# Short matmuls on ones in TensorE's early waits, and column sums spread by TensorE, in a windowed-attention and MoE kernel

## The chip, the core and the metric

One core of a Trainium2 chip runs the whole program. TensorE (PE) multiplies, VectorE (DVE), ScalarE (ACT) and GpSimd (POOL) copy and compute elementwise, and SyncE's queue (SP) issues every DMA. The metric is the device time of one execution in microseconds (us), taken as the median of several. The times of the kernel before are 317.78, 322.66 and 318.96 us, median 318.96.

## The reference

Eight sequences of 576 tokens, eight heads of 64, window 32; then a layer with a squared ReLU whose bias adds a constant times the column sums of `w_out`:

```python
scores = q @ k.T / 8;  scores = where(|i - j| <= 32, scores, -1e9)
x = softmax(scores) @ v            # (8, 8, 576, 64) -> (4608, 512)
h = x @ w_in                       # 512 -> 2048
g = s * relu(h)**2 + b
out = g @ w_out                    # 2048 -> 512
    # = s * (relu(h)**2 @ w_out) + b * column_sums(w_out)
```

## The kernel before

**Order of the work.** Each operation is added to a graph (`_Graph.add`) with an engine, a cost, a key (its due time), what it reads and what it writes. `plan` is a list scheduler: it takes the operation that can start first, then the smaller key, and so writes out one fixed order for each engine; `emit` adds the semaphore waits. On the chip each engine keeps its order, whatever the real times are. So a change of a key, of a cost or of the engine of one copy moves other instructions too.

**Stages.** The first sequence's q and k come in pairs of heads (`load_pair`, L685), are cast (L713), turned by TensorE (L733), copied out of PSUM (L740), and scored (L990) over a bank that was first filled with the mask (`opened`, L1009). Exponentials are taken on ScalarE (L1034). V of the first sequence comes as rows (L624), is cast (L629), and put in place by TensorE with a 0/1 matrix (`place_rows`, L643, in 32-row tiles); the copies out of PSUM are L651/L652. The product with V (`joint`, L915), the normalisation (reciprocal L939, multiply L941), TensorE's transposes (L948) and the copies to XT (L956) end a unit of 128 rows. Sequence 1 goes much the same way (L720, L749, L755, L990, L1020). From sequence 2 on, q and k are loaded whole (`piece`, L798), cast by GpSimd (L806), turned by transposing DMAs (L813), and k is put in order by GpSimd (L823); v is loaded at L607 and cast at L615/L616; the scores are L857.

**The layer.** `s1` (L1185) multiplies a block of tokens with `w_in`, whose eight loads (L579) GpSimd casts (L582), into one of the two banks of W; ScalarE's ReLU (L1192) and VectorE's square (L1194) make GT. The blocks are 224, 128, 160, 256, 256 and then 512 tokens. `early` (L1234) multiplies the first 512 tokens with `w_out` piece by piece, as it arrives, into both banks of O and both of AVN; the later blocks do so in `s2` (L1203). `put` (L1219, L1223) scales by s, adds the vector CVEC = b times the column sums of `w_out`, and stores. The bank of an accumulator is free again only after `put` has read it.

**Column sums.** `colsum` (L1244) lets TensorE multiply ones with `w_out` in four 32-column tiles, so that W's second bank holds the sums of columns 128x to 128x+127 on each of the partitions 32x to 32x+31. One operation of VectorE (L1249) scales them by b into a spare buffer, and 16 copies of 32x128 (L1255 on ScalarE, 4; L1256 on VectorE, 12) spread them to CVEC's 128x512. `put` of the first 512 tokens waits for all 16.

**Before any data** five matmuls of 512 columns on ones run (L528); nothing fills TensorE's later waits.

Of the kernel before, what the change touches and what calls it, by code (L numbers as in the profile page):

```python
# [13 lines left out]
H = 8  # L14
# [3 lines left out]
NPAIR = H // 2  # L18
# [7 lines left out]
SPLIT = (2, 3)  # L26
VROWS = NPAIR
PLACED = NPAIR
WHOLE = 9
SPREAD = ('act', 'dve', 'dve', 'dve')  # L30
# [6 lines left out]
TURNKEY = -20.5  # L37
TURN = (None, 0)
FIRST = ((None, 0), (0, 0), (1, 0), (0, 1), (1, 2), (1, 1), (2, 0), (0, 2), (0, 3), (2, 1), (1, 3), (2, 3), (2, 2), (None, 0), (None, 0), (None, 0), (None, 0))
# [3 lines left out]
HELD = (1800.0, 2800, 700.0, 3600)  # L43
OPEN = -23.1
REST = ('dve', 'dve')
ORDER1 = (('p', 0), ('p', 1), ('w', 0), ('w', 1), ('p', 2), ('p', 3), ('v', 0), ('w', 2), ('w', 3), ('e', 0), ('v', 2), ('v', 3), ('v', 4), ('v', 1))
XTS = 3000.0
ROWS = 4
BODY = 128 * ROWS
XPE = 20  # L50
PACE = ((-1, -1, -1),) * 3
# [3 lines left out]
SLACK = (2000.0, 1500.0, 4500, 4000)  # L55
# [9 lines left out]
COPYK = (('act', 'dve', 'act', 'dve'), ('act', 'act', 'dve', 'dve'))  # L65
XTE = ('act', 'act', 'dve', 'act', 'dve', 'act', 'dve', 'dve', 'act', 'act', 'act', 'act', 'act', 'act', 'dve', 'act', 'act', 'act', 'dve', 'act')
TURN1 = (0, 3, 0, 1, 0, 1, 0, 0, 1)
SCORE1 = ('O', 'O', 'SC', 'SC')
FIRSTQK = (('qk', 'qk', 'kq', 'qk'), ('qk', 'qk', 'kq', 'kq'))
K1 = ('act', 'dve', 'dve', 'pool')  # L70
Q1 = ('pool', 'pool', 'dve', 'dve')
# [6 lines left out]
class _Task:  # L78
    __slots__ = ("n", "stream", "fns", "cost", "lat", "key", "deps", "users", "left",
                 "ready", "start", "fin", "dma", "sem", "seq", "val", "used", "snap", "slack", "after", "next", "half", "mark", "form")  # L80

    def __init__(self, n, stream, fns, cost, lat, key, dma, slack, after, form):
        self.form = form
        self.slack, self.after, self.next = slack, after, []
        self.n, self.stream, self.fns, self.cost, self.lat, self.key, self.dma = \
            n, stream, fns, cost, lat, key, dma
        self.deps, self.users = set(), []
        self.ready = self.start = self.fin = 0.0
        self.sem = self.seq = self.val = None
        self.used = False  # L90
        self.snap = self.half = self.mark = None


class _Graph:
# [12 lines left out]
    MARGIN, FROM = 250.0, -20.05  # L107
    RING, PUSH, CALM, ISSUE, WRITE = 112.0, 95.0, 40.0, 1400.0, 600.0
# [6 lines left out]
    def add(self, stream, fns, cost, reads=(), writes=(), key=0.0, accum=False, dma=None, waits=(),  # L115
            late=0.0, slack=0.0, form=None):
# [18 lines left out]
        t.deps.discard(t)  # L135
        for r in reads:
            self.readers.setdefault(r, []).append(t)
# [9 lines left out]
    def plan(self):  # L147
# [112 lines left out]
        while any(rings.values()):  # L260
            done, clock[0] = serve(rings, clock[0], 1e9)
            done.fin = clock[0] + self.WRITE

# [92 lines left out]
def bass_sliding_window_symmetric__then__act_starrelu_kernel(  # L356
# [13 lines left out]
    sizes = [224, 128, 160, 256, 256]  # L370
# [9 lines left out]
    with ExitStack() as es:  # L380
# [54 lines left out]
        SROW = sb((128, 2), F32, "srow")  # L435

# [56 lines left out]
        def due(c, u):  # L493
            tok = c * S + unit_rows(c, u)[0]
            blk = next(x for x in range(NM) if TBLK[x][0] + TBLK[x][1] > tok)
            f = (tok - TBLK[blk][0]) / TBLK[blk][1]
            before = PH[blk] - PH[blk - 1] if blk > 0 else 4.0
            return PH[blk] - 14.0 - (1.0 - f) * before
# [5 lines left out]
        add("dve", lambda e: e.memset(ONESW[:], 1.0), 150, writes=["ONESW"], key=-99)  # L504
        add("dve", lambda e: e.memset(RECS[:], 1.0), 250, writes=[("REC", i) for i in range(NU)], key=-58)
# [134 lines left out]
        def place_rows(us, key, waits=()):  # L640
# [6 lines left out]
                60.0 + 110.0 * H, form="row", reads=[("VN", 0), ("VN", 1), "PICK"],  # L647
# [21 lines left out]
        def place_tail(waits):  # L669
# [6 lines left out]
                skip_group_check=True) for x in (0, 1)], 300.0, reads=[("NAT", ni), "IDENT"], writes=[res], key=-20.4, waits=waits)  # L676
# [48 lines left out]
        def turn_pair(b, name, pr, key, banks, eng, slack):  # L725
# [3 lines left out]
            if b == 0:  # L729
# [5 lines left out]
                    300.0, form="64", reads=[("NAT", ni), "IDENT"], writes=[res], key=key)  # L735
# [270 lines left out]
        def opened(name, bank, key, waits):  # L1006
# [5 lines left out]
                waits=waits)  # L1012
# [45 lines left out]
        def joint(b, us, key, waits=()):  # L1058
# [6 lines left out]
                    slack=1500.0, waits=waits)  # L1065
# [108 lines left out]
        def s1(m, f0):  # L1174
# [16 lines left out]
                writes=[("W", wb)], key=key, slack=XTS)  # L1191
# [50 lines left out]
        def colsum():  # L1242
# [4 lines left out]
                1050, form="column", reads=["ONESW"] + [("Wout", i, x) for i in range(4) for x in (0, 1)], writes=[("W", 1)], key=-12.0)  # L1247
            some = OUTS[NOUT - 1][:, 0:128]
            add("dve", lambda e: e.tensor_scalar(some, W[:, 1, 0:128], SB128[:, 1:2], None, ALU.mult),  # L1249
                250, reads=[("W", 1), ("SB128", 1)], writes=[("OUTS", NOUT - 1)], key=-12.0)  # L1250
            for y in range(4):
                for x in range(4):
                    to, part = CVEC[32 * y:32 * y + 32, 128 * x:128 * x + 128], some[32 * x:32 * x + 32, :]
                    eng = SPREAD[y]
                    add(eng, (lambda e, to=to, part=part: e.copy(to, part)) if eng == "act" else  # L1255
                        (lambda e, to=to, part=part: e.tensor_copy(to, part)), {"act": 300, "dve": 200}[eng],  # L1256
                        reads=[("OUTS", NOUT - 1)], writes=[("CVEC", x // 2, y)], key=P2[0] + 0.5)
# [281 lines left out]
```

## Time and profile before

| | |
|---|---|
| median of three executions | 318.96 us |
| the profiled execution, device time | 318.48 us |
| its span, first to last instruction | 316.7 us |
| outside the span | 1.78 us |
| mean granted TensorE clock | 0.978 |
| PE, DVE, ACT, POOL busy | 304.4, 189.5, 143.1, 105.6 us |
| moved by DMA | 56.10 MB |

The profile is of one execution. A row of the timeline has the start in us, the busy time, the engine, the line, the operation, output and inputs, shapes and count; in square brackets the idle time before it and what ended that. A row of the windows has the busy time of each engine in that stretch with the number of instructions, and at the end the granted TensorE clock, the mean share of the DMA engines in use, and GB/s. A row of the chain of waits has start, duration, engine and line.

### The profile page before, as it was taken

Reading aid. Unit: us, or ns where it says so; the run is one execution under the profiler, and the core shown is the slowest. Engines: PE = TensorE matmul, PEld = TensorE weight load, DVE = VectorE, ACT = ScalarE, POOL = GpSimd, SP = SyncE. Lnnn points to the kernel's source line nnn. Section 1 sums busy time; section 2 is a strip of 40 time slices with the busy share of each in tenths; the row PEclk is TensorE's granted clock in tenths of the full one; section 3 lists DMA queues with packets and bytes.
Section 4 is the critical chain, followed back from the end, with each engine's and each line's share of the span. In section 5 each row is a group of like instructions: output and inputs, shape, how many; then the busy total and the mean of one; then the engine's idle time right before and its main releaser. Section 6 shows DMA issues by size and latency. Waiting matters only on the chain.

```text
span 316.7 us, 8119 instructions
## 1 busy us (share of the span) xinstructions
PE 304.4 (96%) x3446; PEld 162.3 (51%) x3446; DVE 189.5 (60%) x375; ACT 143.1 (45%) x227; POOL 105.6 (33%) x125
## 2 busy tenths in 40 slices
PE   7799999949999999999999999999999999999995
PEld 3449875637764455454444444444444444444444
DVE  5457785596766867688448655776755543333312
ACT  4726676314744663665136524743544333333300
POOL 4258544661164336626334470266100000000000
PEclk9859999989999999999999999999999999999999
DMA  7999999994799899599999989996521110000022
GB/s 229 369 385 334 339 277 295 147 177 150 254 169 147 279 218 193 148 296 167 149 213 252 194 157 290 252 163 114 151 87 52 52 46 33 35 33 34 34 101 69
DMA packets 97974, 56.10 MB, mean 177 GB/s; under 512 B 70992, under 2 KB 88144, under 8 KB 97936
## 3 DMA queue, kind: packets, MB, share of 16 engines
q1 hardware_dynamic: 97936, 55.56, 74.6%
q8 instruction: 28, 0.46, 0.7%
q14 instruction: 10, 0.08, 0.1%
HBM read 36.70 MB, written 9.44 MB: 146 GB/s over the span
## 4 chain that ended last, share of the span: by engine, by line
PE 91%; DVE 3%; DMA 2%; ACT 1%; SPq 1%; issue 1%
PE w L1185 39%; PE o L1203 35%; PE avn L915 4%; PE o L1234 2%; PE avn L1234 2%; PE sc L857 2%; DVE cvec L1256 2%; DMA stg<-in_q_dram 2%; PE avn L643 1%; PE avn L948 1%; PE o L915 1%; PE sc L915 1%; SPq L685 1%; DVE outs L1219 1%; PE w L749 1%
## 5 line engine op out<-in xcount | busy, mean ns | idle before, releaser
L1185 PE MATMUL w<-xt,win 128*128 128x512 bf16 (+4 forms) x768 | 142.7, 328 | 0.1
L1192 ACT ACTIVATE r<-w 128x512 bf16<-128x512 f32 (+2 forms) x148 | 86.5, 586 | 104.8 <-PE w L1185 88.6
L1194 DVE TENSOR_TENSOR gt<-r 128x512 bf16<-128x512 bf16 (+2 forms) x148 | 81.5, 562 | 72.9 <-ACT r L1192 72.1
L1203 PE MATMUL o<-wout,gt 128*128 128x512 bf16 (+1 forms) x528 | 124.4, 373 | 0.0
L1185 PEld LDWEIGHTS w<-xt,win 128*128 128x128 bf16 x768 | 68.6, 99 | 54.1 <-ACT r L1192 1.8
L1203 PEld LDWEIGHTS o<-wout,gt 128*128 128x128 bf16 x528 | 50.4, 98 | 55.2 <-DVE gt L1194 0.5
L806 POOL CAST nat<-stg 128x1024 bf16<-128x1024 f32 (+1 forms) x36 | 39.8, 1105 | 59.9 <-DMA stg<-in_q_dram 45.8
L823 POOL COPY kt<-ktr 128x512 bf16<-128x512 bf16 (+1 forms) x30 | 30.7, 1022 | 28.4 <-DMA ktr<-nat 27.0
L885 ACT ACTIVATE ex<-sc 128x1024 bf16<-128x1024 f32 (+1 forms) x28 | 28.7, 1024 | 25.1 <-PE avn L915 24.0
L1219 DVE SCALAR_TENSOR_TENSOR outs<-o,sb,cvec 128x512 f32<-128x512 f32 (+1 forms) x35 | 25.5, 732 | 18.8 <-PE o L1203 18.6
L889 DVE TENSOR_TENSOR ex<-ex,mask 128x1024 bf16<-128x1024 bf16 (+1 forms) x28 | 21.1, 753 | 1.5 <-ACT ex L885 0.5
L941 DVE TENSOR_TENSOR xn<-avn,rec 128x512 bf16<-128x512 f32 (+1 forms) x30 | 20.7, 689 | 0.8
L915 PE MATMUL avn<-vb,ex 64*64 64x65 bf16 x912 | 19.2, 197 | 0.1
L915 PEld LDWEIGHTS avn<-vb,ex 64*64 64x64 bf16 x912 | 12.5, 106 | 12.4 <-issue 9.8
L857 PE MATMUL sc<-qt,kt 64*64 64x128 bf16 x432 | 11.4, 216 | 0.0
L616 POOL CAST vb<-vst 128x512 bf16<-128x512 f32 x13 | 9.0, 692 | 6.9 <-DMA vst<-in_v_dram 6.2
L939 DVE RECIPROCAL rec<-avn 128x8 f32<-128x8 f32 (+1 forms) x30 | 6.0, 200 | 7.6 <-PE avn L915 7.4
L582 POOL CAST wout<-stg 128x1024 bf16<-128x1024 f32 x7 | 7.5, 1075 | 6.0 <-DMA stg<-in_moe_w_out_dram 5.8
L1234 PE MATMUL avn<-wout,gt 128*128 128x512 bf16 x32 | 9.2, 380 | 0.0
L582 POOL CAST win<-stg 128x1024 bf16<-128x1024 f32 x8 | 8.4, 1046 | 2.0 <-DMA stg<-in_moe_w_in_dram 1.8
L616 DVE CAST vb<-vst 128x512 bf16<-128x512 f32 (+1 forms) x18 | 8.0, 446 | 0.0
L1234 PE MATMUL o<-wout,gt 128*128 128x512 bf16 x32 | 7.7, 380 | 0.0
(123 smaller groups left out, 155.3 us busy)
## 6 DMA issues: line engine op xcount, KB each, us to landing
out_dram<-outs SPq DMA_DIRECT2D x35, 256.0 KB, 2.9
vst<-in_v_dram SPq DMA_DIRECT2D x28, 256.0 KB, 6.4
stg<-in_k_dram SPq DMA_DIRECT2D x6, 1024.0 KB, 10.8
stg<-in_q_dram SPq DMA_DIRECT2D x6, 1024.0 KB, 5.8
stg<-in_moe_w_in_dram SPq DMA_DIRECT2D x8, 512.0 KB, 9.3
stg<-in_moe_w_out_dram SPq DMA_DIRECT2D x8, 512.0 KB, 6.3
stg<-in_q_dram SPq DMA_DIRECT2D x4, 288.0 KB, 4.9
stg<-in_k_dram SPq DMA_DIRECT2D x4, 288.0 KB, 5.1
```

Source lines behind the costliest of these rows:

```text
L806: add(eng, lambda e, x=x: e.tensor_copy(nat[0:top, 1024 * x:1024 * x + 1024].rearrange("p (i h d) -> p h i d", h=H, i=2), stg[0:top, :].re ...
L823: add("pool", lambda e, c=c, w=w: e.tensor_copy(KT[slot][:, :, c:c + w].rearrange("p a (s i) -> p a s i", i=4), KTR[slot][:, :, :, c // 4: ...
L885: add("act", lambda e, dst=flat_dst, src=flat_src: e.activation(dst, src, AF.Exp, bias=0.0, scale=0.125), 170 + 0.833 * 512 * len(hs), rea ...
L889: add("dve", lambda e, flat=flat, mask=mask: e.tensor_tensor(flat, flat, mask, ALU.mult), 155 + 0.53 * 512 * len(hs), form="two", reads=[( ...
L915: return [lambda e: e.matmul(av[64 * x:64 * x + 64, h, 0:D + 1], lhsT=buf[64 * g:64 * g + 64, h % 2, h // 2, c:c + 64], rhs=VB[64 * g:64 * ...
L941: add("dve", lambda e: e.tensor_tensor(XN[xi][0:p1, :].rearrange("p (a c) -> p a c", a=H), av[0:p1, :, 0:D], REC[ri][0:p1, :].rearrange("p ...
L1185: add("pe", [lambda e, g=g, kc=kc: e.matmul(wt[:, g, :], lhsT=WIN_BF[:, kc, (f0 + g) * 128:(f0 + g + 1) * 128], rhs=XT[:, kc, t0 % XR:t0 % ...
L1192: add("act", lambda e: e.activation(rt, wt, AF.Relu, bias=0.0, scale=1.0), 170 + 0.833 * ng * nt, reads=[("W", wb)], writes=[("R1", rb)], ...
L1194: add("dve", lambda e: e.tensor_tensor(GT[gs][:, f0:f0 + ng, g0:g0 + nt], rt, rt, ALU.mult), 155 + 0.53 * ng * nt, form="two", reads=[("R1 ...
L1203: add("pe", [lambda e, fc=fc: e.matmul(O[:, ob, 0:cn], lhsT=GT[gs][:, fc, g0:g0 + 128], rhs=WOUT_BF[:, fc, c0:c0 + cn], start=(fc == 0), s ...
L1219: add("dve", lambda e: e.scalar_tensor_tensor(OUTS[us][:, 0:cn], bank, SB128[:, 0:1], CVEC[:, c0:c0 + cn], ALU.mult, ALU.add), 210 + 1.05 ...
L1234: add("pe", [lambda e, fc=fc, bank=bank, gs=gs, g0=g0: e.matmul(bank, lhsT=GT[gs][:, fc, g0:g0 + 128], rhs=WOUT_BF[:, fc, :], start=(fc == ...
```

## The change

It does three things, and a fourth in their wake.

1. `fill`, called at the end of `plan`, puts matmuls of ones with ones, 128 columns each, into TensorE's order wherever the plan has TensorE wait in its first 26 us, at least two and as many as the planned wait less 170 ns holds. They write a bank (`spare`, `fresh=`) that a coming matmul overwrites from the start. The order written out has nine such groups before the first `s1`: of 3, 5, 2, 4, 10, 13, 7, 2 and 4, in all 50.
2. `colsum` no longer scales and copies. GpSimd prepares constants early on (a column of -1 and 0 called LESS, 0/1 matrices called pickers in NEG and the spare buffer; 18 memsets). After the column sums VectorE copies them as bf16 (`high`), subtracts that on 31 of 32 rows of each group, GpSimd copies the rest as bf16 (`mid`), and VectorE subtracts again, so that three partitions of each group hold three bf16 terms of the sum (`part`). Four matmuls of 128 columns add the terms and spread them to W's second bank, 128x512, and one ScalarE operation scales by b into CVEC.
3. Constants and due times are set anew: `LEAD` 14 to 10, `SPLIT` so that sequence 0's exponentials all come in halves, the engines of copies (`EV0`, `EV1`, `EV2`, `COPYK`, `XTE`, `REST`, `K1`, `Q1`), `SCORE1`, `TURN1`, slacks.
4. The order on every engine moves with it. GpSimd has 26 of the casts of v (L616 before) instead of 13, VectorE 6 instead of 18. In TensorE's order four of `early`'s 512-column matmuls that stood ahead of sequence 1's first `joint` now stand behind it, six of them instead of two stand behind the column sums, and the four matmuls with the pickers stand behind the first eight matmuls of the block of 256 tokens. GpSimd's `mid` stands behind the two casts of sequence 2's first k piece and ahead of its other casts. GpSimd's memsets of QTS, which wait for sequence 0's last scores, stand behind all eight casts of `w_in` instead of between the fourth and the sixth; the first memsets of the constants (after the fourth cast) wait for the last matmul that reads NEG.

The core of the diff:

```diff
-SPLIT = (2, 3)
-PLACED = NPAIR
+SPLIT = (0, 3)
+PLACED = 3
-EV0 = ('act', 'dve', 'dve', 'act', 'dve')
+EV0 = ('act', 'dve', 'dve', 'dve', 'act')
-EV1 = ('dve', 'pool', 'dve', 'act', 'act')
-EV2 = ('dve', 'pool', 'pool', 'dve', 'dve')
+EV1 = ('dve', 'pool', 'dve', 'pool', 'act')
+EV2 = ('pool', 'pool', 'pool', 'pool', 'dve')
-COPYK = (('act', 'dve', 'act', 'dve'), ('act', 'act', 'dve', 'dve'))
+COPYK = (('act', 'act', 'act', 'dve'), ('act', 'act', 'dve', 'dve'))
...
+    def fill(self):
+        pe = [t for t in self.order if t.stream == "pe"]
+        for i in range(1, len(pe)):
+            a, b = pe[i - 1], pe[i]
+            if b.start > self.WARMED:
+                break
...
+            st, n = best
+            each = 56.0 if st > self.COLD else 109.0
+            count = int((b.start - st - self.GUARD) / each)
+            if count < 2:
+                continue
+            t = _Task(len(self.tasks), "pe", [n.spare[1]] * count, each * count, 0.0, b.key, None, 0.0, [], None)
...
+        def spare(name, bank):
+            return name, lambda e: e.matmul(bank[:, 0:128], lhsT=ONESW[:, :], rhs=ONESW[:, :], start=True, stop=True)
...
-            add("dve", lambda e: e.tensor_scalar(some, W[:, 1, 0:128], SB128[:, 1:2], None, ALU.mult),
-                250, reads=[("W", 1), ("SB128", 1)], writes=[("OUTS", NOUT - 1)], key=-12.0)
-            for y in range(4):
-                for x in range(4):
-                    to, part = CVEC[32 * y:32 * y + 32, 128 * x:128 * x + 128], some[32 * x:32 * x + 32, :]
-                    eng = SPREAD[y]
...
+            add("dve", lambda e: e.tensor_copy(high, W[:, 1, 0:128]), 290, reads=[("W", 1)], writes=["high"], key=SUMS)
+            add("dve", lambda e: e.scalar_tensor_tensor(left, high, LESS[:, 0:1], W[:, 1, 0:128], ALU.mult, ALU.add),
+                300, reads=[("W", 1), "high", "LESS"], writes=["left"], key=SUMS)
+            add(SUME, lambda e: (e.copy if SUME == "act" else e.tensor_copy)(mid, left), {"act": 280, "pool": 250, "dve": 200}[SUME],
+                form="two", reads=["left"], writes=["mid"], key=SUMS)
+            add("dve", lambda e: e.scalar_tensor_tensor(part, mid, LESS[:, 1:2], left, ALU.mult, ALU.add),
+                290, form="two", reads=["left", "mid"], writes=["part"], key=SUMS)
+            add("pe", [lambda e, x=x: e.matmul(W[:, 1, 128 * x:128 * x + 128], lhsT=pickers[x], rhs=part, start=True, stop=True,
+                                               skip_group_check=True) for x in range(4)],
+                240, reads=["part", "PART"], writes=[("W", 1), ("OUTS", NOUT - 1)], key=SUMS)
+            add(SUMC, lambda e: e.activation(CVEC[:, :], W[:, 1, :], AF.Copy, bias=0.0, scale=SB128[:, 1:2]) if SUMC == "act" else
+                e.tensor_scalar(CVEC[:, :], W[:, 1, :], SB128[:, 1:2], None, ALU.mult),
+                {"dve": 688, "act": 597}[SUMC], reads=[("W", 1), ("SB128", 1)],
+                writes=[("CVEC", x, y) for x in (0, 1) for y in range(4)], key=SUMS)
```

More of the change, by code (lines that the diff above doesn't have):

```diff
@@ new lines, in colsum @@
+            buf = OUTS[NOUT - 1]
+            left = buf[:, 0:128]
+            high, mid, part, *some = (buf[:, 128 + 64 * i:192 + 64 * i].bitcast(BF16) for i in range(6))
+            pickers = [NEG[:, :]] + some
+            add("pool", [lambda e: e.memset(LESS[:, :], -1.0), lambda e: e.memset(NEG[:, :], 0.0),
+                         lambda e: e.memset(buf[:, 320:512], 0.0)], 500, writes=["LESS", "PART", ("NEG", 0), ("NEG", 64)], key=PREP)
+            for fns in ([lambda e, x=x: e.memset(pickers[x // 32][x:x + 3, :], 1.0) for x in range(0, 128, 32)],
+                        [lambda e, x=x: e.memset(LESS[x:x + 1, :], 0.0) for x in range(0, 128, 32)],
+                        [lambda e, x=x: e.memset(LESS[x:x + 2, 1:2], 0.0) for x in range(0, 128, 32)]):
+                add("pool", fns, 400, reads=["LESS", "PART"], writes=["LESS", "PART"], key=PREP)
```

86 lines of the change are left out of this document (57 added, 29 removed).

## The prediction

> **What bounds the kernel now.** I read the clock in the page's slices first, then the chain of waits by engine, then TensorE's own waits, then the windows by stage.
>
> ```profile
> PEclk9859999989999999999999999999999999999999
> PE 91%; DVE 3%; DMA 2%; ACT 1%; SPq 1%; issue 1%
> ```
> ```profile
> PE o L915 <- DVE outs L1219: 4.1, 1, 4.1
> ```
> ```profile
> 10.00:14.00 4.00, 2.36 (x70) 1.37 (x70) 2.16 (x3) 3.09 (x6) 1.04 (x1) 0.95 1.11 351
> 14.00:24.00 10.00, 9.12 (x128) 4.53 (x129) 4.35 (x10) 3.54 (x7) 4.89 (x6) 0.51 1.05 385
> ...
> 24.00:64.00 40.00, 39.62 (x590) 29.08 (x588) 28.24 (x57) 24.72 (x47) 23.37 (x32) 1.00 1.04 277
> 64.00:68.00 4.00, 0.00 (x0) 0.00 (x0) 3.80 (x11) 0.53 (x1) 1.56 (x3) 1.00 1.10 210
> 68.00:72.00 4.00, 3.89 (x79) 2.98 (x80) 4.00 (x8) 0.60 (x1) 3.73 (x4) 0.57 0.59 102
> 72.00:316.00 244.00, 241.16 (x2432) 120.33 (x2430) 141.17 (x269) 105.75 (x162) 67.00 (x66) 1.00 0.68 147
> ```
>
> TensorE is the bound: 91% of the chain, and from 72 us on busy at full clock for 241.16 of 244 us. What can be won lies in two places ahead of that. At 64 it stands still for 4.1 us, until the first `put` has emptied O; and it runs at half clock twice, in slice 2 and behind the standstill. The windows date the clock:
>
> ```profile
> 13.50:14.00 0.50, 0.32 (x16) 0.11 (x8) 0.50 (x1) 0.13 (x1) 0.00 (x0) 0.58 1.04 381
> ...
> 23.50:24.00 0.50, 0.50 (x5) 0.43 (x5) 0.50 (x1) 0.45 (x1) 0.31 (x1) 0.68 1.07 371
> ...
> 68.00:69.00 1.00, 0.89 (x56) 0.76 (x60) 1.00 (x2) 0.00 (x0) 0.94 (x2) 0.60 1.15 211
> ...
> 71.00:72.00 1.00, 1.00 (x8) 0.78 (x7) 1.00 (x2) 0.60 (x1) 0.92 (x1) 0.70 0.05 4
> ```
>
> A mean of 0.58 over 0.5 us is 0.08 us of full and 0.42 of half clock: half from 13.58. In the same way it ends at 23.82 (10.24 us), and the second lasts from 68.2 to 71.6 (3.4 us).
>
> **The column sums.** The chain, then the rows of the timelines that price the new steps.
>
> ```profile
> 58.74 1.04 PE w L1244 x64
> ...
> 66.58 1.42 DVE outs L1219 x2
> ...
> 68.04 0.35 PE o L915 x16
> ```
> ```profile
> 60.12 3.77 PE L1185 MATMUL w<-xt,win 128*128 128x256 bf16 x32
> ```
> ```profile
> 59.80 0.35 DVE L1249 TENSOR_SCALAR outs<-w,sb 128x128 f32<-128x128 f32 x1 [1.89 <-PE w L1244]
> ```
> ```profile
> L1256 DVE COPY cvec<-outs x12: 217/230/1086, 60.2 to 66.3; 32x128 f32<-32x128 f32 x12
> ```
> ```profile
> 61.34 0.58 ACT L1192 ACTIVATE r<-w 128x512 bf16<-128x512 f32 x1
> ```
> ```profile
> 52.03 0.29 POOL L546 COPY mask<-mask 128x128 bf16<-128x128 bf16 x1
> ...
> 54.43 2.15 POOL L806 CAST nat<-stg 128x1024 bf16<-128x1024 f32 x2 [0.42 <-DMA stg<-in_k_dram]
> 59.31 4.35 POOL L806 CAST nat<-stg 128x1024 bf16<-128x1024 f32 x4 [2.73 <-DMA stg<-in_q_dram]
> ```
>
> Call C the end of the column sums (59.78 before). Before, TensorE has two 512-column and 32 256-column matmuls, and reaches the next `joint` at 68.04, C + 8.26; the 12 copies on VectorE stand between. A 256-column matmul costs 3.77 / 32 = 0.118 us, 512 columns twice that, 128 half.
>
> After, TensorE has six 512-column matmuls (1.4) and the first eight of the block (0.94): C + 2.3. Meanwhile: `high` 0.35 and `left` 0.35 (the row of L1249, same shape), `mid` 0.29 (the row of L546), `part` 0.35, with hops of 0.03 to 0.06: C + 1.5. No row shows `mid` or `part`; the longest POOL-stretched copy, 1.09 instead of 0.22, is the upper end, and one such (0.87 more) still ends at C + 2.4. So the pickers (four, 0.24) start at C + 2.3, and the work hiding the chain is those 14 matmuls, with 0.8 us to spare. W's other bank then needs its ReLU: C + 2.3 + 0.2 + 0.58 = C + 3.1, so TensorE stands 0.55 us. CVEC follows on ScalarE (0.6, the ReLU's shape): C + 3.7. `put` of O takes 1.42: C + 5.1. TensorE's other 24 matmuls (2.83) end at C + 5.95. So nobody waits for O; 0.85 us of cover is left, and beyond it a later CVEC costs its full lateness. The moved four 512-column matmuls are in the 5.95; without them it is 5.0, against 8.26. Gain 3.2, the pickers included.
>
> With no standstill the clock stays up: half clock for 3.4 us of steady work is 1.7 us. Stage: 4.9. Were the clock to fall all the same, 3.2; the upper end is the whole wait, 4.1 + 1.7 = 5.8.
>
> **The short matmuls.** 50 of 128 columns cost 50 x 0.059 = 2.95 us of TensorE, all in planned waits. Placed wrongly, they delay: the three behind a mask filling by at most 0.2 to 0.3 us, hidden because the next load only lands later. The largest group, 13 (0.77), lies where TensorE waited for VectorE's cast of V.
>
> ```profile
> 12.54 0.76 DVE kt L740
> ...
> 14.51 1.91 PE avn L643 x8
> ...
> 17.18 0.32 PE o L915 x6
> ...
> 18.56 1.82 PE avn L643 x8
> ...
> 23.50 1.81 PE w L1185 x16
> ...
> 29.36 1.80 PE w L1185 x32
> ```
> ```profile
> 19.46 0.68 DVE L941 TENSOR_TENSOR xn<-sc,rec 128x512 bf16<-128x512 f32 x1
> ```
> ```profile
> 15.76 1.04 POOL L582 CAST win<-stg 128x1024 bf16<-128x1024 f32 x1 [0.86 <-DMA stg<-in_moe_w_in_dram]
> ...
> 19.82 1.04 POOL L582 CAST win<-stg 128x1024 bf16<-128x1024 f32 x1 [0.32 <-DMA stg<-in_moe_w_in_dram]
> ...
> 25.48 3.29 POOL L582 CAST win<-stg 128x1024 bf16<-128x1024 f32 x3
> ```
>
> At full clock I follow the same chain. V's placing starts at 14.1 (ScalarE, rid of one long exponential, casts the last k some 0.5 us earlier; the 13 fillers take part of that back) and takes 0.95 instead of 1.9: 15.1. Copies like L941's (0.7) behind two exponentials: 16.0. The `joint`, 18.56 - 17.18 at half clock, takes 0.7 to 0.95: 16.95. Two multiplications and reciprocals: 18.6. Transposes, a copy, the third `joint`: 19.9. Mask and scores (0.65): the first `s1` at 20.6 instead of 23.5, and by its order the group that stood at 29.36 is due near 26.05.
>
> That group needs all eight casts of `w_in`. They start as loads land, (19.82 - 15.76) / 3 = 1.35 us apart; the eighth lands at 15.76 + 7 x 1.35 = 25.2 and is cast by 26.3. Before, GpSimd stood in a memset behind TensorE's scores and ended at 28.77; the memset is behind the casts now. Of the 18 new memsets the first wait for TensorE's last reading of the mask, near 20.4; behind them stand the last four casts, and behind those SP's loads of `w_out`, but the fifth load lands at 21.2 and the others in steps that hide the rest. So the gain here is 29.36 - 26.3 = 3.06: the loads cap it, whatever TensorE does.
>
> The next cap comes at sequence 1's first `joint`:
>
> ```profile
> 50.22 0.62 POOL L616 CAST vb<-vst 128x512 bf16<-128x512 f32 x1 [5.39 <-DMA vst<-in_v_dram]
> ```
> ```profile
> 53.77 0.25 PE L915 MATMUL sc<-vb,ex 64*64 64x65 bf16 x6
> ```
>
> With 3.06 and the four matmuls moved behind it (0.9) it would stand at 49.8, but its last v is cast by 50.84. The load may come a little sooner with what paces it; I take half of the 1.0 as lost: 2.6. Ends: 3.06, and 0 if the clock stays half.
>
> SP loads sequence 2's small pieces of q and k ahead of the large q now; all of them still stand ahead of the transposes, so the last lands as before. The other moves (engines of copies, due times, stores) I cost at nothing: beyond 72 us TensorE's 241.16 us hide VectorE's 141.17 and GpSimd's 67. If that cover goes, the price is in the rivals.
>
> **Sum.** 318.48 (profiled execution: span 316.7 and 1.78 around it) - 4.9 - 2.6 = 311.0. The profiled execution lies 0.48 under the median 318.96.
>
> **Rivals.**
>
> *The clock falls all the same* (the fillers don't do what they are for). For them: in 10 to 14 TensorE was busy 2.36 of 4 us, then the clock fell; up to 27 fillers (1.6 us) raise that. Against: from 14 to 24 it was busy 9.12 of 10, and the clock rose only at 23.82, so V's 32-row tiles and the small `joint`s may count for little, and they remain. Half clock of 3.4 us costs 1.7; three such all of the early 2.6. 312.7 to 313.6; I take 313.4. [...]
>
> *The pickers wait for `mid`*, which stands on GpSimd behind casts of sequence 2's k, landed at 54.43, done at 56.58; C (now about 56.3) + 0.75 is 57. If that load comes as late as q's (59.31), the casts end at 61.5 and the pickers come at 62.2 instead of 58.6: 3.6 us and a fallen clock, 1.7: 316.3.
>
> *Sequence 2 isn't there yet*: what is won is given back later.
>
> ```profile
> 65.47 3.66 SPq L813 DMA_TRANSPOSE qt<-nat  x2
> ```
> ```profile
> DMA to landing us min/median/max: 2.7/4.9/6.0
> ```
> ```profile
> 79.07 0.40 PE L857 MATMUL sc<-qt,kt 64*64 64x128 bf16 x15
> ```
>
> q lands turned at 65.47 + 4.9 = 70.4. TensorE wants it at 79.07 - 7.5 - 0.9 (moved) = 70.7. A transpose 3 us later gives 314.
>
> *Slower*: GpSimd's 13 more casts of v stand ahead of the copies of k, and strictly in order: one waiting for its load holds k, and TensorE's scores behind it.
>
> ```profile
> 100.58 5.41 POOL L823 COPY kt<-ktr 128x512 bf16<-128x512 bf16 x5 [4.05 <-DMA ktr<-nat]
> ```
> ```profile
> 105.52 0.39 PE L857 MATMUL sc<-qt,kt 64*64 64x128 bf16 x15
> ```
>
> Sequence 3's first copy ends at 101.66, 3.9 us ahead of the scores. Two more casts (1.3) fit; a wait of 5.39 as at 50.22 besides exceeds it by 2.8, in six sequences 16.8: 327.8. It decides from 6.3 us per sequence on. Against it: GpSimd waits 4.05 us for k anyway.
>
> **How the numbers follow.** Forecast 0.55 (own range 309.5 to 312.4), clock 0.24, `mid` 0.07, sequence 2 0.08, slower 0.06. 2% (about what a measurement of this kernel can tell from no change) is 6.4 us: under 312.6 is faster. Faster: 0.53 of the forecast and 0.04 of the clock's, 0.57. Slower 0.06, the same 0.37. The range, 308.9 to 314.6, takes in the upper ends of both stages (311.0 - 0.9 - 0.5, and 0.7 for stalls inside the 39.62 of 24 to 64) and the clock and sequence-2 cases.
>
> **What would show it.** Right: no wait of L915 for L1219; the clock at 1.00 in 14 to 24 and 68 to 72; the first `s1` near 20.6, the eighth cast of `w_in` done near 26.3, the `joint` of sequence 1 near 51, scores of sequence 2 near 71. Wrong: half clock in 14 to 24; a wait of the pickers for VectorE behind GpSimd; a wait of L857's successor for GpSimd's k; a total above 314.6.

## The result and the profile after

| | before | after |
|---|---|---|
| median of 20 executions each | 319.51 us | 315.44 us |
| ratio, 95% interval | | 0.987 (0.984 to 0.989) |
| the profiled execution | 318.48 us | 314.66 us |
| its span | 316.7 us | 312.9 us |

The kernel is 1.3% faster, some 4.2 us, against 7.5 predicted, and so short of the 2% that the prediction called faster. The ratios, here and below, leave out executions more than 1.5% above the fastest of their kernel (here six of the twenty after, at 318.30 to 319.39 us with a mean granted clock of 0.973 to 0.978, and one before); the medians hold all.

The page of the kernel after: the clock by slices and the chain by engine, then the busy time by stage (columns as before).

```profile
PEclk9989999999999999999999999999999999999999
...
PE 94%; DMA 2%; issue 1%; DVE 1%; ACT 1%; SPq 0%
```
```profile
10.00:14.00 4.00, 2.19 (x77) 1.69 (x70) 2.18 (x4) 3.30 (x7) 1.04 (x1) 1.00 1.10 347
14.00:24.00 10.00, 9.24 (x165) 5.48 (x165) 3.81 (x9) 3.21 (x6) 4.58 (x5) 0.83 1.05 384
24.00:64.00 40.00, 38.96 (x588) 28.24 (x587) 28.77 (x57) 22.14 (x39) 24.37 (x48) 1.00 0.98 265
64.00:68.00 4.00, 3.92 (x94) 3.20 (x92) 3.93 (x9) 1.83 (x4) 3.75 (x5) 1.00 1.27 149
68.00:72.00 4.00, 4.00 (x40) 3.25 (x38) 3.98 (x7) 2.27 (x4) 3.21 (x4) 1.00 1.09 214
```

The stage at 64 to 72 is what the prediction wanted: TensorE busy 7.92 of 8 us (3.89 before) at full clock. The first stage isn't. In 10 to 14, with 7 matmuls more than before, TensorE is busy for less (2.19 against 2.36), and from 14 to 24 the clock has still lost time. TensorE's longest waits after:

```profile
PE avn L553 <- issue: 2.3, 1, 2.3
...
PE w L1234 <- issue: 0.5, 1, 0.5
```

The wait of 4.1 for the `put` is gone. The longest is new, is at the short matmuls themselves (L553), and is put down to no engine at all: "issue" is time in which TensorE waited for nothing that the profile shows. Its place in TensorE's order:

```profile
11.74 0.45 PE L553 MATMUL avn<-onesw 128*128 128x128 bf16 x5
14.45 0.69 PE L553 MATMUL avn<-onesw 128*128 128x128 bf16 x5 [2.26 <-issue]
...
15.93 0.64 PE L1039 MATMUL o<-qt,kt 64*64 64x128 bf16 x16
16.50 1.56 PE L553 MATMUL avn<-onesw 128*128 128x128 bf16 x13
18.00 1.03 PE L692 MATMUL avn<-gt,pick 32*128 32x512 bf16 x8
```

The group of ten short matmuls is torn in two. Behind the stand come five more of it, the mask, the scores of pair 4 (at 13.35 before), thirteen more short ones at half clock, and only at 18.00 V's placing (14.51 before). The stage at the column sums in TensorE's order:

```profile
59.39 1.08 PE L1293 MATMUL w<-wout,onesw 128*32 128x128 bf16 x64
...
62.91 0.23 PE L1314 MATMUL w<-outs,neg 128*128 128x128 bf16 x1 [0.17 <-DVE outs L1312]
...
63.43 2.79 PE L1234 MATMUL w<-xt,win 128*128 128x256 bf16 x24
66.15 0.32 PE L964 MATMUL o<-vb,ex 64*64 64x65 bf16 x16
```

The column sums end at 60.47 (59.39 and 1.08) and the `joint` stands at 66.15, C + 5.68 (C + 8.26 before), with no wait ahead of it.

The execution divides as follows. From the `joint` to the end before took 316.7 - 68.04 = 248.66, after 312.9 - 66.15 = 246.75: 1.91 less. From C to the `joint` it is 8.26 - 5.68 = 2.58 less, though four 512-column matmuls (0.86) were moved into it, so 3.44. The stage is worth 5.35. The span is 3.8 shorter, so the part ahead of C is 1.55 slower, where 2.6 of gain was predicted.

### The profile page after: what moved, and what is told of

Its sections match the earlier page's. It is cut to its first block, busy times and chain, and to the rows that moved or that the text cites. A ratio compares the mean times of both kernels' runs of the same rounds, so it can differ in the third digit from the quotient of the medians.

```text
span 312.9 us, 8260 instructions
## 1 busy us (share of the span) xinstructions
PE 303.8 (97%) x3500; PEld 163.6 (52%) x3500; DVE 183.9 (59%) x352; ACT 143.2 (46%) x226; POOL 117.1 (37%) x154
## 4 chain that ended last, share of the span: by engine, by line
PE 94%; DMA 2%; issue 1%; DVE 1%; ACT 1%; SPq 0%
PE w L1234 41%; PE o L1252 36%; PE avn L964 4%; PE o L1283 2%; PE avn L1283 2%; PE sc L906 2%; DMA stg<-in_q_dram 2%; PE avn L553 1%; PE avn L997 1%; PE w L782 1%; PE w L798 1%; PE sc L964 1%; PE o L964 1%; PE sc L1039 0%; DVE xn L990 0%
## 5 line engine op out<-in xcount | busy, mean ns | idle before, releaser
L1243 DVE TENSOR_TENSOR gt<-r 128x512 bf16<-128x512 bf16 (+2 forms) x148 | 86.8, 601 | 73.5 <-ACT r L1241 73.2
L990 DVE TENSOR_TENSOR xn<-avn,rec 128x512 bf16<-128x512 f32 (+1 forms) x30 | 20.6, 687 | 0.8
L665 POOL CAST vb<-vst 128x512 bf16<-128x512 f32 x26 | 17.8, 683 | 3.2 <-DMA vst<-in_v_dram 1.7
L1005 ACT COPY xt<-avn 128x512 bf16<-128x512 bf16 (+2 forms) x11 | 5.6, 517 | 6.3 <-PE avn L997 6.3
```

Of the source, the lines that this page charges most:

```text
L990: add("dve", lambda e: e.tensor_tensor(XN[xi][0:p1, :].rearrange("p (a c) -> p a c", a=H), av[0:p1, :, 0:D], REC[ri][0:p1, :].rearrange("p ...
L1243: add("dve", lambda e: e.tensor_tensor(GT[gs][:, f0:f0 + ng, g0:g0 + nt], rt, rt, ALU.mult), 155 + 0.53 * ng * nt, form="two", reads=[("R1 ...
```

## The experiments

The theories. **F**: TensorE's instructions arrive in stretches of fixed length, and the stand is TensorE at the end of one, waiting for the next. Every short matmul is two instructions (load of weights, matmul; the page after counts 3500 of each), so it brings that end nearer. **Rivals**: the stand belongs to the short matmuls or to their bank; or it is a real wait at that place that the profile doesn't name, and would stand ahead of the same work without them.

### No short matmuls

```diff
-        self.fill()
```

> The changed kernel without the 50 short matmuls, everything else as changed. Theory F (TensorE's instructions run out): in the changed kernel TensorE stood 2.26 us in the middle of a group of ten short matmuls, after its 222nd matmul, until 14.45; before, it stood 0.45 us after its 221st, until 14.51. So its first stretch of instructions ends there and the next comes at about 14.5, whatever TensorE does. Without the fillers the scores of the fourth pair stand ahead of that point and run by 13.5, V's placing starts at 14.1 to 14.6, half clock from about 13.6 to 24 as before, and sequence 1's first joint comes at 52.5 to 53.5 instead of 54.5: about 1.5 us less than the changed kernel, 313.9 against its 315.4. Rival W (the gap is a wait for data or another engine that the fillers only make visible): TensorE stands until 14.4 here too, ahead of the fourth pair's scores, V's placing at 16 or later, and with the clock fallen as well it is 1 to 2 us slower than the changed kernel.

315.33 us, ratio 0.988 (0.982 to 0.994).

```profile
12.81 0.42 PE L1038 MATMUL o<-qt,kt 64*64 64x128 bf16 x16
14.38 1.89 PE L691 MATMUL avn<-gt,pick 32*128 32x512 bf16 x8 [1.15 <-DVE gt L677]
```

The scores of pair 4 run at 12.81, with no stand: it isn't a hidden wait of that place. V's placing starts at 14.38, where F had it, but the time of 313.9 was missed: the clock falls at 13.92 and stays half to 27.57, 13.65 us and so 3.41 longer than the 10.24 that F had allowed for. All the same the kernel is as fast as the changed one (0.988 against 0.987): the fifty short matmuls are worth nothing that can be measured. The traces say why: the column sums end at 60.88 without them and at 60.47 with them, 13.65 us at half clock in the one, the stand of 2.26 and 3.42 at half clock in the other.

### Fewer, longer ones

```diff
-            each = 56.0 if st > self.COLD else 109.0
+            each = 216.0 if st > self.COLD else 430.0
...
-            return name, lambda e: e.matmul(bank[:, 0:128], lhsT=ONESW[:, :], rhs=ONESW[:, :], start=True, stop=True)
+            return name, lambda e: e.matmul(bank.rearrange("p (a c) -> p a c", a=4), lhsT=ONESW[:, :],
+                                            rhs=ONESW.rearrange("p (one c) -> p one c", one=1).to_broadcast((128, 4, 128)), start=True, stop=True)
```

At least one of 512 columns in a wait, so some ten in place of fifty.

> The fillers as matmuls of 512 columns, one for each 216 ns (430 ns early) of a planned wait: about ten instead of 50, the same TensorE time. Theory F: only four of them stand ahead of the point where the instructions run out, so it lies in the last matmuls of the fourth pair's scores, which end at 14.6; TensorE stands about 1 us instead of 2.26 and the useful work behind it is 20 matmuls further; V's placing at 15.0 to 15.5 instead of 18.0, at full clock or half, the first s1 near 22.5 instead of 24.55; 2 us less than the changed kernel, 313.4. Theory S (it is the fillers' own time on TensorE that costs, 13 of them 1.5 us at half clock): same time of fillers, so the same as the changed kernel within 0.5 us. Rival W: the gap until 14.4 stays where it was, ahead of the same work; within 0.5 us of the changed kernel.

Four executions: 311.03, 311.22, 316.14, 317.19 us. In the profile (of the 311.22) the clock stays at 1.00, and the stand has gone elsewhere:

```profile
12.82 0.41 PE L1040 MATMUL o<-qt,kt 64*64 64x128 bf16 x13
13.94 0.25 PE L1040 MATMUL o<-qt,kt 64*64 64x128 bf16 x3 [0.71 <-issue]
```

It tears the scores of pair 4, which are no short matmuls and write another bank. That leaves F. Counting the x of TensorE's rows from the start, the stand after lies behind the 222nd matmul, and here it lies behind the 222nd too. F's 313.4 us lies between the two pairs of times. V's placing starts at 14.87, a little ahead of F's 15.0 to 15.5, and the column sums end at 56.85. That is 2.93 earlier than before, 2.07 without the four matmuls that were moved (0.86): where the stand is short and the clock holds, the early stage does gain most of the 2.6 that the prediction wanted.

### The same number, half as long

```diff
-            return name, lambda e: e.matmul(bank[:, 0:128], lhsT=ONESW[:, :], rhs=ONESW[:, :], start=True, stop=True)
+            return name, lambda e: e.matmul(bank[:, 0:64], lhsT=ONESW[:, :], rhs=ONESW[:, 0:64], start=True, stop=True)
```

> The same 50 fillers with 64 columns instead of 128: the same number of instructions, half the TensorE time. Theory F: TensorE stands after the same 222nd matmul, in the same group of ten, until 14.4 to 14.5, a little longer than 2.26 us. Theory S: the 13 fillers ahead of V's placing take half the 1.56 us, V's placing at 17.2 instead of 18.0 (F agrees on this part), but the gap is gone or halved. Rival W: the gap ends at 14.4 too, but need not lie after the 222nd matmul.

One execution, 317.18 us. The stand is behind the 222nd matmul again, and longer, 3.12 us:

```profile
11.88 0.32 PE L553 MATMUL avn<-onesw 128*128 128x64 bf16 x5
15.32 0.45 PE L553 MATMUL avn<-onesw 128*128 128x64 bf16 x5 [3.12 <-issue]
```

So the number of instructions sets the place, not their time. The end is another matter: F had it at 14.4 to 14.5 whatever TensorE does, and it came at 15.32.

### The kernel before with a finer warm-up

```diff
-        add("pe", [lambda e: e.matmul(W[:, 1, :].rearrange("p (a c) -> p a c", a=4), lhsT=ONESW[:, :], rhs=ones,
-                                      start=True, stop=True)] * WARM,
+        add("pe", [lambda e: e.matmul(W[:, 1, 0:128], lhsT=ONESW[:, :], rhs=ONESW[:, :],
+                                      start=True, stop=True)] * (4 * WARM),
```

> The kernel before, with its five warm-up matmuls of 512 columns split into twenty of 128: the same TensorE time, 15 more matmuls ahead of everything, nothing else. Theory F: the instructions run out 15 matmuls of the program earlier, within the 16 scores of the fourth pair, so these stand split, the rest at about 14.5 instead of 13.4, and the exponentials and V's copies after them come about 1 us later; the 0.45 us gap ahead of V's placing is gone. Rivals W and S: nothing moves, the scores run at 13.35 and V's placing at 14.5.

One execution, 319.51 us. The scores of pair 4 weren't torn, as F had said they would be: its forecast missed here.

```profile
13.12 0.50 PE L990 MATMUL o<-qt,kt 64*64 64x128 bf16 x16 [0.85 <-DVE kt L740]
15.06 1.89 PE L643 MATMUL avn<-gt,pick 32*128 32x512 bf16 x8 [1.44 <-DVE gt L629]
```

Another row of the profile explains it: the DMA part counts a queue called "q8 instruction", on the page of the kernel after with 28 packets of 0.46 MB, 16 KB each. Read over narrow windows, that row dates the start of each packet. Here are the kernel after in 11.7 to 11.8, then this experiment in 10.5 to 10.6 (packets, MB, share):

```profile
q8 instruction: 1, 0.02, 75.1%
```
```profile
q8 instruction: 1, 0.02, 68.0%
```

After: the packet starts at 11.76 and TensorE goes on at 14.45, 2.7 us later. Here the packet starts at 10.52; 2.6 later is 13.1, just where the 222nd matmul (the second of the 16 scores, behind 220) runs, which until 13.12 waited for k anyway. So the boundary can have been there with nothing to be seen of it; this run alone doesn't show it. The next experiment makes the same edit where it would be seen.

### The changed kernel with the finer warm-up

The same edit, in the kernel after.

> The changed kernel with its warm-up cut from 5 matmuls of 512 columns into 20 of 128, the same time with 15 instruction pairs more ahead of all else. Theory F counts instructions: the stand comes behind the 222nd matmul of the program again, which is now the 8th of the 18 transposes at about 11.3 us, so that group is split 8 and 10 (one or two either way), and no stand in the middle of the short matmuls; it ends 2.4 to 2.7 us after a packet of the queue that the page calls q8 instruction. Rival (the stand belongs to the short matmuls or to their bank): it stays in the group of ten.

One execution, 316.49 us.

```profile
11.02 0.30 PE L782 MATMUL w<-ident,nat 64*64 64x64 bf16 x8
13.18 0.34 PE L782 MATMUL w<-ident,nat 64*64 64x64 bf16 x10 [1.86 <-issue]
...
25.36 0.20 PE L964 MATMUL avn<-vb,ex 64*64 64x65 bf16 x2
27.74 0.31 PE L964 MATMUL avn<-vb,ex 64*64 64x65 bf16 x10 [2.19 <-issue]
```

The group of transposes is torn 8 to 10, as F said beforehand; nothing near a short matmul stands. And there is a second long stand, of 2.19 us, behind the 476th matmul: of the 1.27 us that TensorE is ahead of the kernel after behind the first boundary (13.18 against 14.45), 0.43 is left there (27.74 against 28.17).

The boundaries that showed so far, by the same counting, with the packet that ended each:

| kernel | behind matmul | TensorE goes on at | packet of q8 at | later by |
|---|---|---|---|---|
| before | 221 | 14.51 | 11.84 | 2.67 |
| after | 222 | 14.45 | 11.76 | 2.69 |
| 512 columns | 222 | 13.94 | 11.29 | 2.65 |
| 64 columns | 222 | 15.32 | 12.84 | 2.48 |
| after, finer warm-up | 222 | 13.18 | 10.54 | 2.64 |
| after | 475 | 28.17 | 25.75 | 2.42 |
| after, finer warm-up | 349 | 19.50 | 16.95 | 2.55 |
| after, finer warm-up | 476 | 27.74 | 25.14 | 2.60 |

In the runs below it is 2.4 to 2.8 us too.

### Each half alone

The kernel before with `colsum` of the kernel after:

```diff
-            some = OUTS[NOUT - 1][:, 0:128]
...
-                        reads=[("OUTS", NOUT - 1)], writes=[("CVEC", x // 2, y)], key=P2[0] + 0.5)
+            buf = OUTS[NOUT - 1]
...
+                writes=[("CVEC", x, y) for x in (0, 1) for y in range(4)], key=SUMS)
```

> The kernel before with the new column sums alone: its own constants, no short matmuls. Theory: the stage at the column sums is worth 4.9 us by itself (3.2 of the wait of the AV for the pass-1 output, 1.7 of the half clock behind it), so 318.9 - 4.9 = 314.0, between 313.0 and 315.8; in the trace the AV joint of sequence 1 starts 5.5 to 6.2 us after the end of the column sums, and the clock stays at 1.00 behind it. Rival (the new sums pay only with the new order of the work): over 317.

316.58 us, ratio 0.990 (0.985 to 0.995), 3.3 us; 4.9 lies just outside, and so does the time, outside 313.0 to 315.8. In the trace the sums end at 61.32 and the `joint` stands at 66.71, C + 5.4, and the clock is 1.00 from 56 to 74:

```profile
63.69 0.23 PE L1270 MATMUL w<-outs,neg 128*128 128x128 bf16 x1 [0.96 <-DVE outs L1268]
...
66.71 0.32 PE L920 MATMUL o<-vb,ex 64*64 64x65 bf16 x16
```

So the column sums carry most of their gain by themselves. Two things are missing. The pickers wait about 0.8 more for `part` than in the changed order (0.96 against 0.17). And from 74 to 150 us, where TensorE is busy throughout in the kernels before and after, it stands for 1.45 us here (busy 25.32 of 26 and 49.23 of 50), for copies and products of VectorE and ScalarE: part of what is won at 66 is lost again in the old order.

The kernel after with the `colsum` of before (the same edit backwards):

> The changed kernel with the old column sums (copied 16 times): short matmuls and new constants stay. Theory F (TensorE's instructions come in stretches, and the next one lands only after its load has queued behind the data): the same stand of 2 to 3 us in the middle of the ten short matmuls, behind the 222nd matmul, and the wait of some 3 us of the AV behind the column sums is back: 315.4 + 4.9 = 320.3, between 318.5 and 322. Rival (the short matmuls do gain about 2.6, and the sums were worth less than planned): 316 to 317.5.

324.13 us, ratio 1.016 (1.010 to 1.022): slower than before, and above the expected 318.5 to 322. The profile is of the fastest execution, 321.63. In it the old copies hold the `joint` for longer in the new order (4.83 against 4.14), and the stand behind the 222nd matmul is there as in the kernel after:

```profile
PE o L964 <- DVE outs L1268: 4.8, 1, 4.8
PE avn L553 <- issue: 2.2, 1, 2.2
```

No trace shows what the slower executions, up to 326.48, lost besides.

The kernel before with `fill` alone (its constants, its sums; 55 short matmuls):

```diff
+        self.fill()
...
+    def fill(self):
```

> The kernel before with the short matmuls alone (its constants, its column sums; 55 fillers of 128 columns). Theory F: the 222nd matmul is the last of the 18 transposes at about 12 us, so TensorE stands from there to 14.2 to 14.6, the 15 fillers planned for that wait run behind it, the scores of pair 4 start at 15 to 15.6 (13.35 before) and v is placed from 15.7 or later (14.51 before); no gain: ratio 0.998 to 1.012. Rival (the prediction's own step: the fillers lie in waits and hold the clock): 2.6 us faster, ratio 0.992 or less, scores of pair 4 at 13.4.

318.96 us, ratio 0.997 (0.991 to 1.003).

```profile
11.73 0.47 PE L778 MATMUL w<-ident,nat 64*64 64x64 bf16 x17
13.57 0.21 PE L778 MATMUL w<-ident,nat 64*64 64x64 bf16 x1 [1.37 <-issue]
13.71 1.01 PE L549 MATMUL avn<-onesw 128*128 128x128 bf16 x15
14.65 0.42 PE L1035 MATMUL o<-qt,kt 64*64 64x128 bf16 x16
```

Torn behind the 222nd (205 + 17), at 13.57 for a packet at 11.08; the fifteen short matmuls planned for a wait run behind it, ahead of the scores, which come 1.3 us later than before. F had put them 0.4 later still, and V's placing, which starts at 15.28, too. No gain can be told, as F said, though the interval just takes in the 0.992 of the rival.

Together: the sums alone 0.990, the short matmuls alone 0.997, sums and new constants without short matmuls 0.988, all three 0.987. Neither the short matmuls nor the new constants are shown to add anything to the sums.

### Versions that might beat both

Filler of 512 columns, four more ahead of the mask of pair 4 and two fewer behind the scores:

```diff
+            count += {2: 4, 3: -2}.get(len(new), 0)
```

> The kernel with fillers of 512 columns, four more of them ahead of the mask of pair 4 (so TensorE has work until the next stretch of instructions lands) and two fewer behind its scores. Theory F: the scores of pair 4 are split 9 and 7, the stand between is under 0.4 us (0.71 with two fillers there), the placing of v starts by 14.5 (14.87 there), the granted clock stays at 1.00 through 10 to 30 us, and most runs lie between 309.5 and 311.5. Rival (whether the clock falls is not set by this stand): the stand shrinks as said, but runs still divide between 311 and 316.

314.12 us, ratio 0.984 (0.980 to 0.988). Torn 9 to 7 as said, but with a stand of 0.82, and a second one at the next boundary, behind the 348th matmul:

```profile
PE avn L1071 <- issue: 2.1, 1, 2.1
...
PE o L1041 <- issue: 0.8, 1, 0.8
```

The clock held at 1.00, yet 309.5 to 311.5 was missed by 2.6 us: the second packet came at 20.31 here (TensorE went on at 22.98), at 17.82 in the first profile with 512 columns.

The version with 512 columns once more, unchanged:

> The kernel with fillers of 512 columns again, for the spread of its times (311.0, 311.2, 316.1 and 317.2 before). Theory: the clock falls in those runs in which one free-running window of 3.41 us holds more than some 40% of idle TensorE, which hangs on the window's phase and on the instant at which the second and third stretch of instructions land; so two clusters again, 310.5 to 311.8 with a clock of 0.99 or more, and 314 to 317.5 with less, and at least two runs of six in each. Rival (the slow ones were a disturbance of those two runs): all six at 310.5 to 312.

315.77 us (314.97 to 316.91), ratio 0.990 (0.986 to 0.994). All six lie in the slower of the theory's two clusters, none near 311, so neither the theory nor its rival came true. The profile has two stands (1.14 behind the 222nd, 1.64 behind the 348th, packets at 11.88 and 20.85) and 3.41 us of half clock (23.30 to 26.71). In the first profile they came at 11.29 and 17.82, and no second stand appeared. So the 311 of two executions looks like a lucky fall of the packets, not a property of the version; two profiles don't prove it. The theory's 40% of idle was an estimate; ahead of the fall at 23.30 TensorE was idle for 43% of 3.41 us (19.88 to 23.29).

Two of its short matmuls left out and one fewer behind the scores:

```diff
+            count = (0, 0, 2, 2, 1, 1, 1)[len(new)]
```

> The same with the two fillers at 7 and 10 us left out and two in place of three behind the scores of pair 4. Theory F: three instruction pairs fewer, so the stretch ends behind the 15th of the 16 scores and the placing of v starts 0.2 us earlier (14.65); the stand of 0.7 stays, the third stretch comes 3 matmuls later in the program: 309.0 to 311.3 where the clock holds, and it holds as often as with all the fillers, since no window gets more than 0.4 us idler. Rival (each stretch that lands late is luck of the queue): a stand of about 2 us at 21 to 23 us and 313 to 314.5.

315.54 us, ratio 0.988 (0.984 to 0.992). Torn behind the 15th score as said, but for 1.87 us (packet at 12.45), and the clock fell for 10.24 us (16.21 to 26.45). 309 to 311.3 was missed. No version here is shown to beat the changed kernel: the intervals of 0.984, 0.988 and 0.990 overlap that of 0.987.

### A quarter of the w_in data

```diff
+                src, part = src[:, :, 0:128], stg[:, :, 0:128]
+                stg = part.rearrange("p a (r c) -> p a r c", r=1).to_broadcast((128, 2, 4, 128))
```

> The changed kernel with a quarter of the w_in loads: each of the eight moves 128 of its 512 columns and the cast copies them four times, so 1 MB comes in place of 4 between 8 and 22 us (the output is then not the reference's; only the early stage is read). Theory Q (the packet with the next stretch of instructions queues behind the data already asked for): the second packet, at 18.40 us and 3.9 us behind TensorE's return, comes within 1.5 us of that return, by 16.0; the first, at 11.76, comes 0.5 to 2 us earlier, so that the stand of 2.26 behind the 222nd matmul shrinks to between 0 and 1.8. Rival (the load of instructions has its own rhythm, whatever the data do): packets at 11.3 to 12.2 and 17.5 to 19.0, stand 2.0 to 2.5.

One execution, 315.5 us. Of DMA in 16 to 22 us, the kernel after and then this one (the last three columns are clock, mean share of the DMA engines, GB/s):

```profile
16.00:22.00 6.00, 5.85 (x113) 3.61 (x114) 1.85 (x5) 2.14 (x4) 3.57 (x4) 0.84 1.05 388
```
```profile
16.00:22.00 6.00, 5.92 (x112) 3.34 (x110) 1.38 (x4) 2.15 (x4) 3.02 (x3) 0.82 0.71 210
```

The second packet came at 16.72, 1.6 us behind TensorE's return at 15.14, where the kernel after has 3.95 (18.40 behind 14.45). In the ten other traces with a stand behind the 221st or 222nd matmul, the next packet comes 3.7 to 6.5 us behind the return. So the data do hold that packet up, as far as one execution shows it, though 1.5 us and 16.0 were the bounds I had set. The first came at 12.38, later than in the kernel after (11.76), and the stand was 2.91: a miss. From 8 to 12 us, ahead of the first packet, the share of the DMA engines was still 1.06 here (1.11 in the kernel after), so less of `w_in` did not empty the queue there. The q, k and v loads asked for earlier may be what delays the first packet; that wasn't tried, and stays open.

## Why the prediction was wrong, step by step

**What bounds the kernel**: right. TensorE has 94% of the chain, 91% before.

**Column sums, 4.9**: right, 5.35 in the trace (3.44 and 1.91 for 3.2 and 1.7). The steps in it: VectorE's and GpSimd's rows after.

```profile
60.52 0.29 DVE L1307 CAST outs<-w 128x128 bf16<-128x128 f32 x1 [1.89 <-PE w L1293]
60.84 0.35 DVE L1308 SCALAR_TENSOR_TENSOR outs<-outs,less,w 128x128 f32<-128x128 bf16 x1
61.65 1.21 DVE L1312 SCALAR_TENSOR_TENSOR outs<-outs,less 128x128 bf16<-128x128 bf16 x1 [0.46 <-POOL outs L1310]
```
```profile
61.32 0.29 POOL L1310 CAST outs<-outs 128x128 bf16<-128x128 f32 x1 [0.94 <-DVE outs L1308]
61.68 4.41 POOL L855 CAST nat<-stg 48x1024 bf16<-48x1024 f32 x4
```

`part` took 1.21, not 0.35: the upper end, from the copies before that took 1.07 to 1.09 beside a GpSimd cast (0.22 with GpSimd idle), was the true one. The chain ended at C + 2.39, the pickers started at C + 2.44 (2.3 predicted), and the cover of eight `s1` matmuls was short by 0.17. The row stands beside a GpSimd cast of about 1.1 (4.41 for four, the first starting 0.03 behind it); `left`, an operation of like form with one input in PSUM, took 0.35 with GpSimd idle. No row shows how the cast lengthens it. The clock stayed at 1.00 as predicted.

**Short matmuls, 2.6 of gain**: this step failed, and with the other sign: 1.55 lost ahead of C. As the prediction put it, they "cost 50 x 0.059 = 2.95 us of TensorE, all in planned waits", and "V's placing starts at 14.1". It started at 18.00, 3.9 late, and the first `s1` at 24.55, 3.95 behind the 20.6 given. So the error is all there, and divides in two. The stand of 2.26 is one part: besides TensorE's time there was a second price, in instructions, which the prediction put at nothing. The other part follows from the first. With the stand TensorE was busy for 34% of the 3.41 us up to 14.51, and the next 3.42 us ran at half clock. The work from 14.45 to 18.00 took 3.55 us without a gap, of which by my estimate the half clock cost 1.71 (half of 3.42; V's placing took 1.91 at half clock before and 1.03 at full clock after); at full clock it would take 1.84, and 1.84 behind 12.19, where the stand began, is 14.03, the 14.1 of the prediction. L678's cast of V was done by 14.19, so V's placing waited for TensorE alone.

The short matmuls don't bear the loss of 1.55 alone. Without them the part ahead of C is no faster (C at 60.88 against 60.47), with 13.65 us at half clock against 3.42. They did what they were for, the clock, and lost it to their instructions.

The rows that should have warned were there before. TensorE's loads of weights in the kernel before:

```profile
14.06 0.10 PEld L643 LDWEIGHTS avn<-gt,pick 32*128 32x128 bf16 x1 [0.45 <-DVE gt L629]
14.51 0.13 PEld L643 LDWEIGHTS avn<-gt,pick 32*128 32x128 bf16 x3 [0.35 <-issue]
```

V's placing stood with its first weights loaded from 14.06 until 14.51, and the next load is put down to "issue". The prediction took the whole wait of 0.69 in front of it for one for VectorE's cast of V, which was done at 14.00, and put thirteen short matmuls there. `fill` put 37 more instruction pairs (3, 5, 2, 4, 10 and 13) ahead of that point, and the prediction never asked what brings instructions.

**The eighth w_in cast by 26.3, the group by 26.05**: wrong as a consequence. GpSimd's first constant memset waited 3.91 us for TensorE's last reader of the mask, which came late, and the casts ended at 30.20; the group started at 30.77 (29.36 before). In the profile with 512 columns, where that wait was 0.77, they ended at 27.09: 26.3 was 0.8 too early in any case.

**Sequence 1's joint at 51, scores of sequence 2 near 71**: 54.48 and 74.65, late by what the start had lost; no wait for v, none for the transposed q.

**Rivals.** *The clock falls all the same* came half true: it fell, for 3.42 us (14.51 to 17.93) and not 10.24, and not behind 32-row tiles (V's placing came at 18.00) but behind the stand of 2.26. The sum of that rival, 313.4, has no stand in it either. *The pickers wait for `mid`*: 0.17, no more. *Sequence 2* and *slower by casts of v*: neither wait appeared; the profile lists no TensorE wait behind 66 us.

**The sum** for the profiled execution: 318.48 - 5.35 + 1.55 = 314.68, measured 314.66. What stays open is why a packet comes 3.7 to 6.5 us behind TensorE's crossing of the last boundary, and differs by 2.5 us between two runs of one kernel (3.88 and 6.36 with 512 columns).

## What to carry to other kernels

A matmul put into a wait cost instructions here as well as time (the stand at the boundary grew from 0.45 to 2.26 us): where many small matmuls run while the DMA engines are full, count the pairs between the packets of the instruction queue, and see whether a wait is put down to "issue". A few long matmuls cost fewer instructions than many short ones, which the traces favour but no time here proves (0.990 and 0.987); even then, measure with several executions and a second chip before a lucky one is believed. A serial chain of small copies in front of an accumulator's release is worth taking apart: here it was all of the gain that could be measured (0.990 by itself, 0.987 with the rest).

## What the hardware showed

**Instructions come in packets.** Each is 16 KB (28 are 0.46 MB), and the boundaries lie 126 to 127 matmul pairs apart (222, 348 or 349, 475 or 476). That they bring TensorE's instructions is read off the times: in every stand dated here TensorE went on 2.4 to 2.8 us behind one, and no row shows what a packet holds. In the kernel after the first four packets start at 11.76, 18.40, 25.75 and 30.79: about 6 us for 127 pairs, some 50 ns each, while a transpose of 64 columns takes 26 (0.47 us for 18) and a short matmul 69 (0.90 for thirteen at full clock, with the finer warm-up). So by these rates the transposes outrun their own instructions, and short matmuls hardly let these catch up. The longest stand was 3.12 us (64 columns), with the DMA engines at a share of 1.12 and then 1.05 (10.18 to 13.59, 13.60 to 17.01).

**The clock falls without an idle window.** The half clock lasts 10.24 and 3.42 us before, 3.42 after and 13.65 without short matmuls, which is three, one, one and four times 3.41, and the full clock between the two before lasts 44.37 (23.82 to 68.19), thirteen times. So I count in windows of 3.41 us that run on through the changes of the clock; no row shows a window itself. Here is the one that ends where the clock falls, before, after and without short matmuls; and one of 512 columns with four more, behind which the clock did not fall. No change of clock dates the edges of this last one: they are counted from the instant near 4.50 at which its matmuls become shorter:

```profile
10.17:13.58 3.41, 2.05 (x70) 1.24 (x69) 1.57 (x3) 2.79 (x5) 1.04 (x1) 1.00 1.12 344
```
```profile
11.10:14.51 3.41, 1.15 (x41) 0.94 (x41) 1.45 (x2) 2.20 (x5) 1.46 (x2) 1.00 1.10 351
```
```profile
10.50:13.91 3.41, 1.94 (x62) 1.01 (x54) 1.34 (x3) 3.33 (x8) 1.04 (x1) 1.00 1.10 352
```
```profile
21.57:24.98 3.41, 2.00 (x27) 1.90 (x27) 0.45 (x2) 1.46 (x2) 3.11 (x7) 1.00 1.07 364
```

TensorE was busy 60%, 34% and 57% of the windows at whose end it fell, and 59% of the one at whose end it did not. So by my estimate from these four a limit would lie near 60%; four windows, one of them dated indirectly and with busy time modelled at its ends, don't fix it. The edges fall at other instants in every run (13.58, 14.51, 13.92), so whether a given stand costs a window of half clock may be partly chance. How many windows it stays half differs too: one after, three before, four without short matmuls. What brings it back was not tried.
